# Reciprocal row sums of an attention kernel: by TensorE transposition, or over DRAM

## The chip, the cores and the metric

The kernel runs on one core of a Trainium2 chip. The metric is the device time of one execution in microseconds. The kernel before takes 977.03 us, the median of 3 runs (976.8 to 977.04).

## The reference

Causal attention with a forget gate over 4 batches, 8 heads, 576 positions and 64 channels a head, and behind it a dense mixture of 4 experts over the 2304 tokens. All is in float32.

```python
scores = scale * np.matmul(q, k.transpose(0, 1, 3, 2))
cum = np.cumsum(np.log(np.clip(f, 0.0001, 1.0)), axis=-1)
scores = np.where(causal, -1e9, scores + cum[:, :, :, None] - cum[:, :, None, :])
attn = np.exp(scores - np.max(scores, axis=-1, keepdims=True))
attn = attn / (np.sum(attn, axis=-1, keepdims=True) + 1e-09)
x = np.matmul(attn, v)                    # then heads side by side: (2304, 512)
p = domain_probs / (domain_probs.sum(-1, keepdims=True) + 1e-09)
for e in range(4):
    out += p[:, e:e + 1] * (np.maximum(x @ w1[e], 0.0) @ w2[e])
```

## The kernel before

**Tiling.** Float32 products are made of three products of parts: every operand is split into a rounded part (float32r, "hi") and its remainder ("lo"). ScalarE makes the rounded part, VectorE or GpSimd the remainder. The attention works on jobs: a job is a batch, a pair of heads and a half of the positions (half 0: the first 256 queries, in two tiles of 128; half 1: the other 320, in three tiles of 128 that begin at 256, 384 and 448, so the last two overlap by 64). There are 32 jobs, in the order of `JOBS` (line 35): batches 0 to 3 of half 0, then batches 0 to 3 of half 1, each with 4 pairs (`pr` 0 to 3). The first 4 jobs (class `First`, line 587) run in a start-up phase whose order is written out by hand (`startup`, line 1064). The other 28 are worked on while the experts' layers already run on the chunks of 256 tokens that are ready.

**Order of the work.** Each job has two heads, and the list `heads` (line 664) runs through all of them. `head_steps(n)` (line 667) lists the steps of stage n: preparation and loads for heads to come, the scores of head n tile by tile (`qk_tile`: TensorE scores, VectorE mask and row minimum of the negated scores, ScalarE exponential with the row sums), between them the transposition of the probabilities of head n-1 (`tr`: TensorE, then ScalarE's rounded copy `tr_hi` and VectorE's remainder `tr_lo`), then the product with the values (`av`). Each step has a cost, and `pace` (line 1052) deals the steps out between the quarters of the experts' steps (`Step.l1`, `Step.l2`) by these costs. Tile's scheduler then orders each engine's instructions; in the start-up phase it keeps the written order.

**The row sums.** When a pair's second head has its exponentials, `recip` (line 420) adds 1e-9 to the row sums and takes the reciprocals on VectorE; GpSimd widens them so that each stands 64 times in a row (`rb`, line 427). At the end of the next stage `fin` (line 549) calls `spread` (line 432): TensorE transposes each tile of `rb` into a PSUM tile from the pool `ps_a`, so that the reciprocal of a query stands in a column over the 64 partitions of each head. `fin` multiplies the pair's result `xs` by it (line 556, or line 579 straight into the chunk's tile `xf`), and for the chunks in `DIRECT` splits it into `xh` and `xl` (lines 562, 565). `First` uses the same `recip` and `spread` through `spread_out` (line 636), which copies the PSUM tile to SBUF.

**Places and buffers.** `place` (line 38) says which columns of a job go to which chunk of 256 tokens. `ps_a` has four slots of one bank; the scores `s`, transposed probabilities `t`, products `o` and spread sums `b` share it. All transfers of the kernel before are issued by SyncE. Lines met below: 377 scores, 391 row minimum, 406 exponential, 422 and 425 sums and reciprocals, 427 widening, 437 spreading, 465 transposition of probabilities, 475 and 482 its two copies, 515 product with the values, 595 and 608 scores and transposition of `First`, 764 and 794 the experts' two layers, 731 and 736 the split of weights, 816 the sum over experts, 914, 934 and 992 the last phase, in which 4 chunks together go through layers with seven products in place of eight (`Big`).

## Time and profile before

| what | value |
|---|---|
| median of the runs | 977.03 us |
| the profiled execution | 976.83 us |
| its span | 975.0 us |
| TensorE clock granted | 0.999 |
| TensorE busy | 963.2 us (99%) |
| VectorE busy | 657.3 us (67%) |
| ScalarE busy | 472.0 us (48%) |
| GpSimd busy | 413.0 us (42%) |
| transfers' share of 16 DMA engines | 26.8% |

The span goes from the first to the last profiled instruction; the execution's time has 1.8 us more around it. In the rows, PE is TensorE's matmuls, PEld its loads of weights into the array, DVE is VectorE, ACT ScalarE, POOL GpSimd and SP SyncE; SPq is SyncE's sequencer, which issues transfers. Records of matmuls overlap: a record's length is not the time that the next one waits. The attention's jobs after the first four take from about 27 to 560 us, the experts' sweeps go on to about 605 us, and then the last phase begins.

### The profile page before, as it was taken

Reading aid. Unit: us, or ns where it says so; the run is one execution under the profiler, and the core shown is the slowest. Engines: PE = TensorE matmul, PEld = TensorE weight load, DVE = VectorE, ACT = ScalarE, POOL = GpSimd, SP = SyncE. Lnnn points to the kernel's source line nnn. Section 1 sums busy time; section 2 is a strip of 40 time slices with the busy share of each in tenths; the row PEclk is TensorE's granted clock in tenths of the full one; section 3 lists DMA queues with packets and bytes.
Section 4 is the critical chain, followed back from the end, with each engine's and each line's share of the span. In section 5 each row is a group of like instructions: output and inputs, shape, how many; then the busy total and the mean of one; then the engine's idle time right before and its main releaser. Section 6 shows DMA issues by size and latency. Waiting matters only on the chain.

```text
span 975.0 us, 15448 instructions
## 1 busy us (share of the span) xinstructions
PE 963.2 (99%) x5690; PEld 848.1 (87%) x5690; DVE 657.3 (67%) x1349; ACT 472.0 (48%) x979; POOL 413.0 (42%) x459
## 2 busy tenths in 40 slices
PE   8999999999999999999999999999999999999998
PEld 6898999899999999999899999988788888888886
DVE  6876565777867878877777563247866666566665
ACT  7776665566556656666556353234333232323220
POOL 4987763502303202204104083477654444555410
PEclk9999999999999999999999999999999999999999
DMA  7665331332412212313412022322211112111002
GB/s 258 255 207 163 118 106 49 103 109 69 137 52 90 102 54 84 120 52 96 150 57 66 23 66 83 113 86 66 87 44 44 44 43 69 62 44 44 23 0 87
DMA packets 29819, 85.87 MB, mean 88 GB/s; under 512 B 3160, under 2 KB 5264, under 8 KB 29744
## 3 DMA queue, kind: packets, MB, share of 16 engines
q1 hardware_dynamic: 29744, 84.89, 26.8%
q8 instruction: 45, 0.74, 0.3%
q14 instruction: 30, 0.25, 0.1%
HBM read 80.00 MB, written 4.87 MB: 87 GB/s over the span
## 4 chain that ended last, share of the span: by engine, by line
PE 87%; POOL 4%; DVE 3%; issue 2%; DMA 2%; ACT 1%; POOLq 0%; ACTq 0%; DVEq 0%
PE l L764 21%; PE l L794 20%; PE y L992 17%; PE m L934 13%; PE s L377 5%; PE t L465 5%; PE o L515 5%; POOL bwl L914 2%; DMA wr<-in_w 1%; POOL wt L891 1%; PE b L437 1%; POOL wl L736 1%; DVE kl L333 1%; DVE hi L339 0%; ACT wh L731 0%
## 5 line engine op out<-in xcount | busy, mean ns | idle before, releaser
L736 POOL TENSOR_TENSOR wl<-wr,wh 128x512 fp32r<-128x512 f32 x114 | 150.3, 1344 | 76.6 <-ACT wh L731 63.0
L764 PE MATMUL l<-xl,wh 128*128 128x256 f32 x640 | 182.0, 285 | 0.3 <-DVE xl L658 0.3
L764 PE MATMUL l<-xh,wh 128*128 128x256 f32 x640 | 181.2, 284 | 0.2 <-ACT xh L657 0.2
L764 PE MATMUL l<-xh,wl 128*128 128x256 f32 x640 | 181.3, 284 | 0.0
L816 DVE SCALAR_TENSOR_TENSOR acc<-y,prob,acc 128x512 f32<-128x512 f32 x120 | 88.3, 746 | 68.5 <-PE y L992 68.5
L406 ACT ACTIVATE p<-p,nm 128x576 f32<-128x576 f32 (+2 forms) x160 | 96.0, 600 | 64.8 <-DVE nm L391 64.3
L794 PE MATMUL l<-wh,gh 128*128 128x512 f32 x320 | 127.2, 398 | 0.0
L794 PE MATMUL l<-wl,gh 128*128 128x512 f32 x320 | 127.1, 397 | 0.0
L794 PE MATMUL l<-wh,gl 128*128 128x512 f32 x320 | 126.0, 396 | 0.0
L764 PEld LDWEIGHTS l<-xh,wh 128*128 128x128 f32 x640 | 120.5, 188 | 3.2 <-ACT xh L657 0.4
L764 PEld LDWEIGHTS l<-xl,wh 128*128 128x128 f32 x640 | 120.6, 188 | 3.0 <-DVE xl L658 0.5
L764 PEld LDWEIGHTS l<-xh,wl 128*128 128x128 f32 x640 | 120.5, 188 | 0.5
L325 POOL CAST q<-raw 64x320 fp32r<-64x320 f32 (+1 forms) x56 | 26.9, 480 | 210.3 <-PE s L377 181.9
L914 POOL TENSOR_TENSOR bwl<-wr,bwh 128x256 fp32r<-128x256 f32 (+1 forms) x80 | 78.5, 1009 | 80.5 <-ACT bwh L911 80.5
L391 DVE CUSTOM_DVE_ANT_0 p<-s,mask 128x288 f32<-128x288 f32 (+2 forms) x160 | 75.6, 477 | 43.3 <-PE s L377 39.7
L992 PE MATMUL y<-bwh,hh 128*128 128x512 f32 x256 | 101.1, 395 | 0.8 <-DVE acc L816 0.8
L992 PE MATMUL y<-bwl,hh 128*128 128x512 f32 x256 | 101.1, 395 | 0.0
L992 PE MATMUL y<-bwh,hl 128*128 128x512 f32 x256 | 100.4, 395 | 0.0
L776 DVE SCALAR_TENSOR_TENSOR gl<-l,gh 128x512 fp32r<-128x512 f32 x80 | 54.9, 686 | 54.6 <-ACT gh L775 54.4
L482 DVE TENSOR_TENSOR ptl<-t,pth 128x320 fp32r<-128x320 f32 (+2 forms) x120 | 65.3, 553 | 37.0 <-ACT pth L475 36.6
L934 PE MATMUL m<-rl,bwh 128*128 128x512 f32 x224 | 87.5, 390 | 0.0
L934 PE MATMUL m<-rh,bwh 128*128 128x512 f32 x224 | 87.3, 390 | 0.0
(117 smaller groups left out, 2077.5 us busy)
## 6 DMA issues: line engine op xcount, KB each, us to landing
wr<-in_w SPq DMA_DIRECT2D x96, 512.0 KB
raw<-in_qk SPq DMA_DIRECT2D x16, 896.0 KB
raw<-in_qk SPq DMA_DIRECT2D x12, 512.0 KB
vr<-in_v SPq DMA_DIRECT2D x16, 320.0 KB
out<-acc SPq DMA_DIRECT2D x16, 256.0 KB
vr<-in_v SPq DMA_DIRECT2D x8, 128.0 KB
first<-in_qk SPq DMA_DIRECT2D x3, 256.0 KB
first<-in_v SPq DMA_DIRECT2D x4, 128.0 KB
```

The lines of the kernel that those rows point to most:

```text
L377: nc.tensor.matmul(out=ps[:, at : at + z - a], lhsT=lhsT, rhs=rhs, start=(m == 0), stop=(m == 1),)
L391: nc.vector.tensor_tensor_reduce(out=pt[:, a:z], in0=ps, in1=mask[:, m0 + a : m0 + z], scale=-0.125, scalar=BIG if n == 0 else nm[:, col : ...
L406: return nc.scalar.activation(out=pt[:, :w_], in_=pt[:, :w_], func=AF.Exp, scale=-1.0, bias=self.nmax[hh][:, c : c + 1], accum_out=self.ss ...
L482: nc.vector.tensor_tensor(out=lo[:, a0 + first : a0 + at - first], in0=ps[:, 2 * first : at], in1=hi[:, a0 + first : a0 + at - first].bitc ...
L736: eng.tensor_tensor(out=wl[n][:, a:z], in0=wraw[n][:, a:z], in1=wh[n][:, a:z].bitcast(F32), op=ALU.subtract)
L764: nc.tensor.matmul(out=self.l1p[:, fi, :], lhsT=lhsT, rhs=rhs[:, k, :], start=(k == 0 and m == 0), stop=(k == 3 and m == 2),)
L776: nc.vector.scalar_tensor_tensor(out=self.gl, in0=self.l1p, scalar=0.0, in1=self.gh.bitcast(F32), op0=ALU.max, op1=ALU.subtract,)
L794: nc.tensor.matmul(out=l2[tt], lhsT=lhsT, rhs=rhs, start=(self.ps == 0 and fi == 0 and m == 0), stop=(self.ps == 1 and fi == 1 and m == 2),)
L816: nc.vector.scalar_tensor_tensor(out=acc[c][:, tt, :], in0=ps, scalar=sc, in1=acc[c][:, tt, :], op0=ALU.mult, op1=ALU.add,)
L914: nc.gpsimd.tensor_tensor(out=lo[:, a:z], in0=x[:, a:z], in1=hi[:, a:z].bitcast(F32), op=ALU.subtract)
L934: nc.tensor.matmul(out=ps, lhsT=lhsT[:, o], rhs=rhs[:, k, :], start=(k == 0 and i == 0), stop=(k == 1 and i == 2),)
L992: nc.tensor.matmul(out=ps, lhsT=lhsT, rhs=rhs, start=(fi == 0 and m == 0), stop=(fi == 1 and m == 2),)
```

## The change

For a pair that is not the last of its group (`pr < NPR - 1`) and that belongs to neither batch 0 nor batch 1 of half 0 (`b + 4 * half > 1`), the flag `far_sums` is set. For such a pair, `recip` ends in `send` in place of `widen`: VectorE writes the reciprocals into a 128x32 tile, turns that in blocks of 32x32, and ScalarE's queue issues a transfer of it to DRAM. After the last block of transposed probabilities of the second head, `fetch` issues on ScalarE's queue a transfer from DRAM that gives every row to the 64 partitions of its head, into an SBUF tile. `fin` comes in the stage after (`head_steps`, behind the first transposition block and the first tile of scores), and multiplies by that tile. The other pairs keep GpSimd's widening and TensorE's transposition; their spread tile now has the third tile of half 1 at columns 256 to 383, so a product that runs over column 256 is made in two instructions (`scale`). `First.spread_out` calls `spread` twice. The words that came with the change speak of 20 of 28 later pairs.

```diff
--- before.py
+++ after.py
@@ -104,6 +104,7 @@
     prob = const.tile([128, NT // 128, E], F32, name="prob")
     psum_ = const.tile([128, NT // 128, 1], F32, name="psum_")
     warm = const.tile([B * H, 1], F32, name="warm")
+    rs32 = [const.tile([128, 32], F32, name=f"rs32_{n}") for n in range(2)]
     ncd = dr_p.tile([B * H, 2, S], F32, tag="ncd", name="ncd", bufs=1)
 
     scr = acc_p.tile([128, 1024], F32, tag="acc", name="scr")
@@ -166,6 +167,8 @@
             channel_multiplier=1,
         )
         make_identity(nc, ident)
+        for t in rs32:
+            nc.gpsimd.memset(t, 1.0)
         for i in jobs[1:NPR]:
             nc.gpsimd.memset(i.kq[64:65, :, :CH], 8.0)
         for t in q2:
@@ -261,6 +264,7 @@
             self.qo, self.ko = (0, CH) if half == 0 else (self.wk, 0)
             self.njt = 2 if half == 0 else 5
             self.nm = f"{b}_{pr}_{half}"
+            self.far_sums = pr < NPR - 1 and b + 4 * half > 1
             self.hi, self.kl, self.p, self.nmax = {}, {}, {}, {}
             self.sp, self.last, self.pt, self.tp, self.op = {}, {}, {}, {}, {}
 
@@ -354,7 +358,6 @@
             if hh == 0:
                 n = len(self.its)
                 self.ssum = st_p.tile([128, 2, n], F32, tag="ssum", name=f"ss{self.nm}")
-                self.rs = st_p.tile([128, 2, n], F32, tag="rs", name=f"rs{self.nm}")
 
         def qk_pe(self, hh, its):
 
@@ -422,22 +425,52 @@
             nc.vector.tensor_scalar(
                 out=self.ssum, in0=self.ssum, scalar1=1e-9, scalar2=None, op0=ALU.add
             )
-            nc.vector.reciprocal(out=self.rs, in_=self.ssum)
+            if self.far_sums:
+                self.send()
+            else:
+                self.widen()
+
+        def widen(self):
+            n = len(self.its)
+            rs = st_p.tile([128, 2, n], F32, tag="rs", name=f"rs{self.nm}", bufs=2)
+            nc.vector.reciprocal(out=rs, in_=self.ssum)
             self.rb = x_p.tile([128, 3, 2, D], F32, tag="r", name=f"rb{self.nm}")
             nc.gpsimd.tensor_copy(
                 out=self.rb[:, :n],
-                in_=self.rs.rearrange("p h i -> p i h").unsqueeze(3).to_broadcast([128, n, 2, D]),
+                in_=rs.rearrange("p h i -> p i h").unsqueeze(3).to_broadcast([128, n, 2, D]),
             )
 
         def spread(self):
 
             ps = ps_a.tile([128, 512], F32, tag="a", name=f"b{self.nm}")
             for t in self.its:
-                i, o = t - self.its[0], TOK0[t] - self.q0
+                i = t - self.its[0]
                 nc.tensor.transpose(
-                    ps[:, o : o + 128], self.rb[:, i].rearrange("p h d -> p (h d)"), ident
+                    ps[:, 128 * i : 128 * i + 128], self.rb[:, i].rearrange("p h d -> p (h d)"), ident
                 )
             self.r = ps
+
+        def send(self):
+            n, x = len(self.its), rs32[self.pr % 2]
+            nc.vector.reciprocal(
+                out=x[:, : 2 * n].rearrange("p (h i) -> p h i", h=2), in_=self.ssum
+            )
+            rt = st_p.tile([128, 32], F32, tag="rt", name=f"rt{self.nm}", bufs=2)
+            nc.vector.transpose(out=rt, in_=x)
+            self.rd = dr_p.tile([32, 4, 32], F32, tag="rd", name=f"rd{self.nm}")
+            nc.scalar.dma_start(out=self.rd.rearrange("c b r -> b c r"), in_=rt)
+
+        def fetch(self):
+            n = len(self.its)
+            self.r = x_p.tile([128, 384], F32, tag="r", name=f"r{self.nm}")
+            with tc.issue_after(self.tail.ins):
+                nc.scalar.dma_start(
+                    out=self.r[:, : 128 * n],
+                    in_=self.rd[: 2 * n]
+                    .rearrange("(h i) b r -> h (i b r)", h=2)
+                    .unsqueeze(1)
+                    .to_broadcast([2, 64, 128 * n]),
+                )
 
         def blocks(self):
 
@@ -472,7 +505,7 @@
 
         def tr_hi(self, hh, gi):
             ps, a0, first, at = self.tp[hh, gi]
-            nc.scalar.activation(
+            self.tail = nc.scalar.activation(
                 out=self.pt[hh][0][:, a0 : a0 + at - first], in_=ps[:, first:at], func=AF.Copy
             )
 
@@ -498,6 +531,8 @@
             self.tr_pe(hh, gi)
             self.tr_hi(hh, gi)
             self.tr_lo(hh, gi)
+            if hh == 1 and gi == len(self.blocks()) - 1 and self.far_sums:
+                self.fetch()
 
         def av_pe(self, hh):
             w_ = self.wq
@@ -551,11 +586,10 @@
             pieces = place(self.b, self.half)
             k = self.pr
             direct = any(p[1] in DIRECT for p in pieces)
-            self.spread()
+            if not self.far_sums:
+                self.spread()
             if direct:
-                nc.vector.tensor_tensor(
-                    out=self.xs[:, :w_], in0=self.xs[:, :w_], in1=self.r[:, :w_], op=ALU.mult
-                )
+                self.scale(self.xs, 0, w_)
             for d, c, o, n in pieces:
                 if c in DIRECT:
                     th, tl = x_tiles(c)
@@ -576,12 +610,17 @@
                             out=xf[c][:, k, o : o + n], in_=self.xs[:, d : d + n]
                         )
                     else:
-                        nc.vector.tensor_tensor(
-                            out=xf[c][:, k, o : o + n],
-                            in0=self.xs[:, d : d + n],
-                            in1=self.r[:, d : d + n],
-                            op=ALU.mult,
-                        )
+                        self.scale(xf[c][:, k, o : o + n], d, n)
+
+        def scale(self, out, d, n):
+            for a, z, o in ((d, min(d + n, 256), 0), (max(d, 256), d + n, 64)):
+                if a < z:
+                    nc.vector.tensor_tensor(
+                        out=out[:, a - d : z - d],
+                        in0=self.xs[:, a:z],
+                        in1=self.r[:, a + o : z + o],
+                        op=ALU.mult,
+                    )
 
 
     class First(Job):
@@ -634,6 +673,7 @@
                 )
 
         def spread_out(self):
+            self.spread()
             self.spread()
             self.rc = x_p.tile([128, 320], F32, tag="tmp", name=f"rc{self.nm}")
             nc.scalar.activation(out=self.rc[:, :CH], in_=self.r[:, :CH], func=AF.Copy)
@@ -691,13 +731,15 @@
             for gi in range(len(j.blocks())):
                 ts.append((500, lambda j=j, hh=hh, gi=gi: j.tr(hh, gi)))
             us.append((200 + 400 * j.half, lambda j=j, hh=hh: j.av(hh)))
-            if hh == 1:
+            if hh == 1 and not j.far_sums:
                 us.append((0, j.fin))
         if n + 1 < len(heads):
             j, hh = heads[n + 1]
             us.append((0, lambda j=j, hh=hh: j.begin(hh)))
         for k in range(max(len(qs), len(ts))):
             st += ts[k : k + 1] + qs[k : k + 1]
+            if k == 0 and n > FIRST + 1 and heads[n - 2][1] and heads[n - 2][0].far_sums:
+                st.append((0, heads[n - 2][0].fin))
         return st + us
```

## Rows read from the trace of the kernel before

**Rows 1.** The page, busy time by engine: us (share of the span) xinstructions.
```profile
PE 963.2 (99%) x5690; PEld 848.1 (87%) x5690; DVE 657.3 (67%) x1349; ACT 472.0 (48%) x979; POOL 413.0 (42%) x459
```

**Rows 2.** Busy time by stretch: stretch, its us, PE, PEld, DVE, ACT, POOL, PEclk, DMA, GB/s.
```profile
98.00:210.00 112.00, 111.29 (x773) 102.97 (x772) 71.67 (x186) 69.13 (x167) 58.63 (x72) 1.00 0.33 100
210.00:560.00 350.00, 349.52 (x2396) 324.07 (x2395) 262.81 (x635) 207.24 (x432) 75.59 (x90) 1.00 0.25 82
```

**Rows 3.** The chain that ended last, 596 to 760 us: start us, us, what.
```profile
603.97 2.08 PE l L794 x9
...
606.08 1.07 ACT wh L731
...
626.47 3.36 DMA wr<-in_w
```

**Rows 4.** Groups by form: busy us, mean ns of one, idle us before.
```profile
L437 PE MATMUL b<-ident,rb 128*128 128x128 f32 x80 | 15.2, 286 | 1.1 <-POOL rb L427 1.1
...
L425 DVE RECIPROCAL rs<-ss 128x6 f32<-128x6 f32 x16 | 3.0, 185 | 0.8
```

**Rows 5.** Timeline of PE, a block of three: start us, us, engine, line, operation.
```profile
248.46 0.55 PE L437 MATMUL b<-ident,rb 128*128 128x128 f32 x3
248.77 0.36 PE L764 MATMUL l<-xh,wl 128*128 128x256 f32 x1
248.97 0.28 PE L764 MATMUL l<-xh,wh 128*128 128x256 f32 x1
...
249.43 0.28 PE L764 MATMUL l<-xh,wl 128*128 128x256 f32 x1
249.55 0.28 PE L764 MATMUL l<-xh,wh 128*128 128x256 f32 x1
```

**Rows 6.** Timeline of PE, a block of two.
```profile
119.34 0.38 PE L437 MATMUL b<-ident,rb 128*128 128x128 f32 x2
119.55 0.38 PE L465 MATMUL t<-ident,p 128*128 128x128 f32 x2
```

**Rows 7.** Timeline of all engines in the start-up phase.
```profile
16.01 0.82 PE L595 MATMUL s<-first 65*128 65x128 f32 x4
...
17.20 0.42 DVE L391 CUSTOM_DVE_ANT_0 p<-s,mask 128x256 f32<-128x256 f32 x1
...
24.02 0.44 PE L437 MATMUL b<-ident,rb 128*128 128x128 f32 x2 [1.05 <-POOL rb L427]
```

**Rows 8.** Timeline of SP, 200 to 330 us: one issue of each kind.
```profile
202.28 0.25 SPq L295 DMA_DIRECT2D kl<-ncd  x1
...
215.91 0.55 SPq L276 DMA_DIRECT2D raw<-in_qk  x1
...
250.64 0.34 SPq L714 DMA_DIRECT2D wr<-in_w  x1
```

**Rows 9.** Timeline of SP at the start: the decay rows to DRAM and back.
```profile
14.55 0.31 SPq L200 DMA_DIRECT2D ncd<-scr  x1
...
20.17 0.53 SPq L295 DMA_DIRECT2D kl<-ncd  x2
```

**Rows 10.** The page, DMA queue: packets, MB, share of 16 engines' span.
```profile
q1 hardware_dynamic: 29744, 84.89, 26.8%
```

**Rows 11.** Timeline of all engines around one pair's sums, half 1, batch 0.
```profile
216.00 0.19 DVE L425 RECIPROCAL rs<-ss 128x6 f32<-128x6 f32 x1
...
217.06 0.62 ACT L406 ACTIVATE p<-p,nm 128x384 f32<-128x384 f32 x1 [1.13 <-DVE nm L391]
...
221.07 0.44 ACT L475 ACTIVATE pth<-t 128x320 fp32r<-128x320 f32 x1 [1.80 <-PE t L465]
...
227.69 0.55 DVE L391 CUSTOM_DVE_ANT_0 p<-s,mask 128x384 f32<-128x384 f32 x1
```

## Prediction

> **What bounds the kernel now.** I read the engines' shares first. TensorE is busy for 99% of the span; no other engine passes 67% [rows 1]. A busy TensorE need not be a bound one, so the next view is the table by stretches. The pairs that the change touches are worked on from about 98 to 560 us. There TensorE misses 0.71 us of 112 and 0.48 us of 350, at a granted clock of 1.00, which is the level of 2.4 GHz [rows 2]. VectorE is busy 64 and 75% of these two stretches, ScalarE 62 and 59%. So in this stage an end comes earlier only by taking work off TensorE, and at most 1.2 us is to be had by taking its waits away. Then I asked whether a gain made there lasts to the end. The chain of waits goes from the stage's last TensorE work at 603.97 into ScalarE's split of a weight at 606.08 [rows 3], and then through GpSimd and weight transfers (626.47): what follows starts when TensorE lets go of a buffer, so it moves forward with TensorE.
>
> **The change, part by part.** By its condition (not a chunk's last pair, and neither batch 0 nor batch 1 of the first half) the far way is taken by 6 groups of pairs times 3, which is 18 pairs and not 20: 6 of the first half with two transpositions each, 12 of the second with three, 48 transpositions in all. The other 10 later pairs and the 4 first ones keep theirs.
>
> *Taken from TensorE.* The record of such a transposition lasts 286 ns [rows 4], but records overlap, so the price is read from starts. In a block of three the first starts at 248.46 and the next matmul at 248.77, 0.31 us later; that matmul then takes 0.20 us to its successor, where the same kind further on takes 0.12 [rows 5]. So a block of three costs 0.31 + 0.08 = 0.39 us. A block of two, with another transposition behind it, costs 119.55 - 119.34 = 0.21 us [rows 6]. Sum: 12 x 0.39 + 6 x 0.21 = 4.7 + 1.3 = 6.0 us, all on the engine that sets the end. The Trainium skill ("TensorE: Matmul & The Clock Gate", Part 4) gives about 275 ns for one 128x128 transposition in a kernel's context; the record agrees and the starts do not, for three start within 0.31 us. By that figure the 48 would be 13.2 us and the time 965; the sum goes by the starts.
>
> *Added at the start.* The four first pairs now transpose twice: 8 more transpositions, and four more PSUM tiles out of the four slots that scores, transposed probabilities and spread sums share. The last of the four blocks starts at 24.02 after TensorE waited 1.05 us for the widened sums from GpSimd, and its 0.2 us lies on the path; the earlier three come out of that wait. If the slots go round in order, a fifth tile in the ring makes the scores that start at 16.01 wait for the slot of the scores before them, which VectorE reads until 17.20 + 0.42 = 17.62 [rows 7]: 1.6 us later. What hides it is again the 1.05 us before the last block, since GpSimd's queue decides when that one starts. Bounds: 0.2 us (all hidden but the last block) to 2.0 us (1.6 beside 0.4). I take 0.4, nearer the lower end, because that wait of 1.05 us is on GpSimd's queue, and its work there doesn't read these scores.
>
> *Moved to ScalarE's queue.* Each far pair issues a store of its 32 columns and a load that copies each row to 64 partitions: 36 issues. The trace has none on ScalarE; on SyncE one takes 0.25 us (the decay rows, 2 partitions), 0.34 us (a weight, 128 partitions) or 0.55 us (raw queries and keys, 128 partitions in two pieces) [rows 8]. So 36 x 0.25 to 0.55, or 9 to 20 us, of ScalarE's time over 460 us. It idles about 40% there, so this is hidden unless it stands in front of something that TensorE needs at once. Behind the store stand the next exponentials; ScalarE already waits 1.13 us at 217.06 for VectorE [rows 11]. Behind the load stand the next gate and exponentials.
>
> *VectorE.* One more instruction a pair, the turning of a 128x32 tile: nearest is the reciprocal of 128x6 at 0.19 us [rows 4]. A second-half product over column 256 is now cut in two, one more short instruction for 16 pairs, priced alike: 34 x 0.19 = 6.5 us, which VectorE's idle quarter covers; but the turning stands between the sums and the next row minimum (216.00, then the exponential at 217.06 [rows 11]), the chain that ends in TensorE's next transpositions. GpSimd loses 18 copies and gains two small fills: nothing on the path.
>
> *What ScalarE and VectorE cost TensorE.* Bounds: nothing (the 1.13 us of ScalarE's waiting in the pair of rows 11 takes the issue in) to the full chain, 0.2 us of turning plus 0.34 us of issue (the weight's, the middle one of rows 8, since store and load have 128 partitions in one piece) for every pair, 18 x 0.54 = 9.7 us. The order of all queues is made anew around the changed instructions and TensorE has other matmuls to put between, as it now does with almost no wait [rows 2], so I take 0.08 us a pair, 1.4 us.
>
> *The product a head later.* It waits for the store, then the load. The nearest row for such a round trip is the decay rows' way over DRAM at the start: store issued at 14.55, its reader not before 20.17, 5.6 us, while transfers were at their densest [rows 9]. The store is issued near 216.2, the load behind the last copy of the next head's transposed probabilities, near 221.5, and the product stands after the first tile of the head after that, near 228.2 [rows 11]. That leaves 6.7 us for the load. No SyncE issue is moved; SyncE's queue is passed by nothing. A chunk's last pair still closes at its old place, so no chunk is ready later.
>
> *Sum.* The profiled execution has a span of 975.0 and 976.83 us in all, 0.2 under the median of 977.03. 976.83 - 6.0 + 0.4 + 1.4 = 972.6; against the median 972.8.
>
> **The rivals.**
>
> *A. ScalarE late, slower.* Place: the store's issue and VectorE's turning between a pair's sums and the next exponentials. Price: the full 0.54 us a pair reaches TensorE: 976.83 - 6.0 + 0.4 + 9.7 = 980.9. It decides from the point where a pair loses more than it gains, 5.6 / 18 = 0.31 us. For it: TensorE issues in order and already runs without a gap, so nothing absorbs a late operand but the order itself. Against it: the 1.13 us of ScalarE waiting right there. Chance 0.15.
>
> *B. The load is late.* Mean packet: 26.8% of 16 x 975 us over 29744 packets is 0.14 us for 2.85 KB [rows 10]. 128 rows over 16 engines are 8 packets, 1.1 us; over two engines 64, 9.0 us. The two-engine end would land the load at 221.5 + 0.3 + 9.0 = 230.8, 2.6 us after VectorE reaches the product; VectorE idles 25% of a head's 11 us, 2.7 us, so most of that is absorbed; a quarter of it, 0.65 us for 12 pairs, adds 7.8 to the 972.6: 980.4. For the two engines speaks the Trainium skill ("DMA: Bandwidth & Descriptors", Rules for kernel authors): an outermost dimension of fewer than 16 confines a transfer to that many engines, and the load's source begins with the 2 heads; no run here shows it for this load. Against the delay: 1.5 KB rows are half the mean packet, so 64 of them take nearer 4.5 us and land before 228. Chance 0.10.
>
> *C. No gain.* The stage ends earlier but the GpSimd and transfer chain from 606 us on [rows 3] holds the old pace: 976.8. Against it, that chain starts from TensorE. Chance 0.10.
>
> *D. More gain.* 18 PSUM tiles fewer in the ring, and the 1.2 us of waits in the stage go too, with no loss on ScalarE: 976.83 - 6.0 + 0.2 - 1.2 = 969.8. Chance 0.13.
>
> *E. The records are the price:* 48 x 286 ns [rows 4] = 13.7 us off TensorE, 964.9 with the rest as forecast. Against it stand the starts of rows 5. Chance 0.02.
>
> *F. Not what it says:* the far pairs are 18, and were they 20, two more blocks of three would add 0.8 us of gain; inside the forecast.
>
> **How the numbers follow.** Forecast 972.8 with 0.50; its own range, with the start at 0.2 to 2.0 and lateness at 0 to 4 us, is 971.0 to 977. A change of 0.2%, 1.95 us, is about what a measurement can tell from none, so faster means under 975.1 and slower over 979.0. Faster: 0.46 of the forecast's 0.50, D and E: 0.61. Within: C's 0.10, 0.04 of the forecast and 0.04 of A's and B's milder shapes: 0.18. Slower: the rest of A and B: 0.21. For 8 in 10 the range goes from D's 969.8 up through the forecast and C to the milder half of A and B, to 980.0.
>
> **What would show each step.** Right: TensorE's record has 40 transpositions of sums (80 now, less 48, plus 8), about 5 us less matmul work between 98 and 560, and its idle there stays under 3 us; 36 transfers on ScalarE's queue at 0.25 to 0.55 us; the load lands within 6 us; the first weight product starts within 0.5 us of its old time. Wrong by A: TensorE idles for several us between 98 and 560 with ScalarE's exponentials or copies named as releasers. Wrong by B: VectorE waits for the load before the product. Wrong by the start: the first layer's matmuls begin over 1 us later. Wrong by C: the attention stage ends 5 us earlier and the end doesn't.

## The result, and the profile after

The changed kernel takes 986.99 us, the median of 4 runs (985.83 to 993.06), against 977.02 before: a ratio of 1.0115 (95% interval 1.008 to 1.0151). It is slower by 10 us, where 972.8 was forecast and the range ended at 980.0. The profiled execution is the longest of these runs (993.06 us, span 991.3), so its rows show where the time goes, and the sizes below come from the ratios.

The page's first part and its row for ScalarE's queue of transfers, to be read beside [rows 1] and [rows 10]:

```profile
PE 971.1 (98%) x5650; PEld 854.1 (86%) x5650; DVE 667.7 (67%) x1383; ACT 470.0 (47%) x979; POOL 405.5 (41%) x443
...
q10 hardware_dynamic: 4716, 3.44, 1.1%
```

TensorE has 40 matmuls fewer (48 transpositions removed, 8 added) and yet is busy 8 us longer. Not all of the 8 us is the change's: in this execution the granted clock was 0.50 in two stretches of 6.8 us, from about 9.5 and from about 135.8 us on, and work at half the clock makes up to 6.8 us of it (an estimate from these two lengths). VectorE has the 34 instructions more that were counted. The queue's 4716 packets are 18 pairs by 262: 128 rows stored, 128 loaded, and 6 that end a transfer, one for each engine that took part. By their records those are four engines for the store and two for the load.

Busy time by stretch, the columns of [rows 2]:

```profile
98.00:210.00 112.00, 105.56 (x708) 97.17 (x708) 77.60 (x206) 71.20 (x178) 59.12 (x69) 0.97 0.33 106
210.00:560.00 350.00, 345.69 (x2333) 319.14 (x2333) 261.60 (x643) 201.68 (x420) 68.44 (x75) 1.00 0.27 91
```

TensorE idles 6.44 and 4.31 us of these stretches, together 10.75, where it idled 1.19 before. It also does less in the same time: 708 matmuls for 773, and 2333 for 2396, though only 12 and 36 were removed from these stages. The groups of the removed and the new work answer to [rows 4]:

```profile
L448 PE MATMUL b<-ident,rb 128*128 128x128 f32 x40 | 7.1, 279 | 0.4 <-POOL rb L438 0.4
...
L459 DVE STREAM_TRANSPOSE rt<-rs 128x32 f32<-128x32 f32 x18 | 3.7, 203 | 0.2
```

So the transpositions did go, 80 to 40. What TensorE and the engines before it waited for, 98 to 605 us (total us, times, longest):

```profile
DVE xf L618 <- DMA r<-rd: 8.0, 5, 2.3
...
PE t L498 <- ACT p L409: 5.8, 5, 2.4
...
ACT p L409 <- DMA rd<-rt: 3.4, 1, 3.4
...
PE s L380 <- DVE xs L572: 2.5, 2, 2.3
ACT gh L817 <- DMA rd<-rt: 2.1, 1, 2.1
...
DVE xs L618 <- DMA r<-rd: 1.6, 2, 0.8
```

The road over DRAM is the way of the sums into DRAM and back, and both halves of it are in the list: `rd<-rt` is the store, `r<-rd` the load. For each, an engine stands that TensorE needs. (The 2.5 us for `xs` L572 are not the road's; the last section comes to them.) Timeline of one store and load of half 0 (ACTq is ScalarE's sequencer):

```profile
114.26 0.56 ACTq L461 DMA_DIRECT2D rd<-rt  x1
...
118.58 0.53 ACTq L467 DMA_DIRECT2D r<-rd  x1
...
119.16 0.40 ACT L409 ACTIVATE p<-p,nm 128x128 f32<-128x128 f32 x1 [3.39 <-DMA rd<-rt]
...
119.71 0.33 PE L498 MATMUL t<-ident,p 128*128 128x128 f32 x1 [1.92 <-ACT p L409]
```

The load may only go out when the store has landed, 4 us after its issue. ScalarE takes its queue in order: it stands 3.39 us, the exponential behind the load is late, and TensorE stands 1.92 us for it. One pair on, the same thing has another name in the list: the exponential at 135.47 waits 3.43 us, put down to a transfer of queries and keys, but the load ahead of it on ScalarE's queue goes out at 134.88, 0.4 us after the last packet of its store. And one of half 1:

```profile
354.98 0.54 ACTq L467 DMA_DIRECT2D r<-rd  x1
...
361.29 0.49 DVE L618 TENSOR_TENSOR xf<-xs,r 128x192 f32<-128x192 f32 x2 [1.74 <-DMA r<-rd]
```

VectorE gets to the product before the load has landed and stands; row minima wait behind it.

The start, beside [rows 7]. The first 27 us by the columns of [rows 2], before and below it after:

```profile
0.00:27.00 27.00, 22.51 (x118) 17.33 (x118) 17.99 (x62) 19.20 (x57) 14.41 (x28) 1.00 0.82 267
```

```profile
0.00:27.00 27.00, 24.02 (x112) 19.57 (x113) 15.82 (x58) 17.85 (x53) 12.21 (x27) 0.87 0.79 250
```

The first spreading and the first weight product before, and the same after with the last two spreadings:

```profile
15.80 0.38 PE L437 MATMUL b<-ident,rb 128*128 128x128 f32 x2
...
24.87 0.36 PE L764 MATMUL l<-xh,wh 128*128 128x256 f32 x1
```

```profile
17.99 0.60 PE L448 MATMUL b<-ident,rb 128*128 128x128 f32 x4
...
25.17 0.60 PE L448 MATMUL b<-ident,rb 128*128 128x128 f32 x4
26.19 0.66 PE L448 MATMUL b<-ident,rb 128*128 128x128 f32 x4 [0.41 <-POOL rb L438]
...
27.25 0.36 PE L806 MATMUL l<-xh,wh 128*128 128x256 f32 x1
```

The first weight product begins at 27.25, 2.4 us later than before. But TensorE comes to its first spreading 2.2 us late (17.99 for 15.80), when nothing has been doubled yet. The granted clock is 0.87 in the mean of these 27 us, where it was 1.00: this is the stretch at 0.50 from about 9.5 us on. So most of the 2.4 us is this execution's clock. A run shown below, with one spreading and the same 0.87 (load and product held), begins its first weight product at 26.75.

### The profile page after: what moved, and what is told of

It is laid out like the page before. It is cut to its first block, busy times and chain, and to the rows that moved or that the text cites. A ratio compares the mean times of both kernels' runs of the same rounds, so it can differ in the third digit from the quotient of the medians.

```text
span 991.3 us, 15453 instructions
## 1 busy us (share of the span) xinstructions
PE 971.1 (98%) x5650; PEld 854.1 (86%) x5650; DVE 667.7 (67%) x1383; ACT 470.0 (47%) x979; POOL 405.5 (41%) x443
## 3 DMA queue, kind: packets, MB, share of 16 engines
q10 hardware_dynamic: 4716, 3.44, 1.1%
## 4 chain that ended last, share of the span: by engine, by line
PE 81%; DVE 5%; DMA 4%; POOL 3%; issue 3%; ACT 2%; ACTq 0%; POOLq 0%; DVEq 0%
PE l L806 19%; PE l L836 19%; PE y L1034 16%; PE m L976 12%; PE s L380 5%; PE t L498 5%; PE o L550 4%; POOL bwl L956 2%; DMA rd<-rt 1%; DMA wr<-in_w 1%; POOL wt L933 1%; DMA r<-rd 1%; DVE rl L920 1%; PE s L634 1%; DVE v L316 1%
## 5 line engine op out<-in xcount | busy, mean ns | idle before, releaser
L976 PE MATMUL m<-rh,bwl 128*128 128x512 f32 x224 | 86.5, 390 | 0.0
```

What stands on the lines that cost most here:

```text
L976: nc.tensor.matmul(out=ps, lhsT=lhsT[:, o], rhs=rhs[:, k, :], start=(k == 0 and i == 0), stop=(k == 1 and i == 2),)
```

## The experiments

Three theories to begin with: **W**, engines stand for the store and the load; **V**, VectorE's new work or the new order of the queues; **S**, the start. Each ratio is against the kernel before on the same chip, with its 95% interval.

**The road and the start, each alone.**

```diff
# no road: store and load out
-            nc.scalar.dma_start(out=self.rd.rearrange("c b r -> b c r"), in_=rt)
...
+            self.r = r_one
# one spread, in the changed kernel
             self.spread()
-            self.spread()
# two spreads, in the kernel before
             self.spread()
+            self.spread()
```

> Left out: the store to DRAM and the load back; the 18 far pairs are multiplied by a constant tile of ones in place of their reciprocals. VectorE's turning, the product a head later, the cut products and the doubled spreading at the start all stay. Theory W (the road over DRAM: ScalarE stands before the load until the store has landed, VectorE stands before the product until the load has landed, TensorE runs dry behind them): 972 to 976 us, TensorE's idle time between 98 and 560 us back from 10.8 to under 3 us. Rival V (VectorE's added instructions and the order made anew are what costs): 983 us or more. Rival S (the doubled spreading at the start): 983 us or more.

Measured: 980.18 us, 1.0024 (1.0013 to 1.0035). The road is some 9 us of the 11, and TensorE's idle time from 98 to 560 us falls to 1.77 us, as W said. V and S alone, at 983 or more, are out. But W's 972 to 976 us are missed: with 48 transpositions fewer and no transfer at all the kernel is still not faster. (The tile of ones lies ahead of other tiles and moves them further; what that does comes below.)

> The changed kernel with one spreading per first pair, as before. W: the first weight product comes back from 27.2 to about 25 us and the time falls by 1 to 4 us, to 983 to 986. Rival S (the doubled spreading delays the start, lets the clock fall and shifts all that follows): 977 us or less. V: 984 to 987.

Measured: 987.58 us, 1.0096 (1.0071 to 1.0121). The first weight product is back at 24.94, but the time is not: W's 983 to 986 are missed as well as S's 977. S is not the cause.

> The kernel before with nothing changed but the doubled spreading of the first four pairs. W and V: 977.5 to 980 us, the first weight product 0.5 to 2.5 us later than at 24.87. S: 984 us or more.

Measured: 979.67 us, 1.0015 (0.9988 to 1.0043). By this run alone the start's doubling is worth -1 to 4 us, too wide to use: one of its ten runs took 990.40 us at a granted clock of 0.931, and the four fastest, 977.01 to 977.47, lie 0.3 to 0.8 us above the fastest of the kernel before (976.70). The first weight product begins at 26.92, but here too TensorE is late ahead of all spreading: eight score matmuls from 9.11 on take 2.90 us, where before they took 1.55. Whether the doubling makes such a slow beginning likelier is not shown.

**The product later, a first attempt.**

```diff
# load a head later, product a further head later
-            if hh == 1 and gi == len(self.blocks()) - 1 and self.far_sums:
-                self.fetch()
+            k = jobs.index(self) - 1
+            if hh == 0 and gi == len(self.blocks()) - 1 and jobs[k].far_sums:
+                jobs[k].tail = self.tail
+                jobs[k].fetch()
...
-                st.append((0, heads[n - 2][0].fin))
+                st.append((0, heads[n - 3][0].fin))
```

> The changed kernel with the load issued one head later (behind the next pair's first head's last copy) and the product one head later again, so that the store has landed long before ScalarE reaches the load, and the load before VectorE reaches the product. All instructions are the same ones. W: 972 to 977 us, no wait of ScalarE over 1 us before a load, TensorE's idle time between 98 and 560 us under 4 us. V and S: 983 us or more.

Measured: 1005.0 us, 1.0277 (1.0246 to 1.0308). The trace of this run says why. First its waits on the load's tile, then one load and the product behind it:

```profile
  DMA r<-rd: 56.8, 17
```

```profile
225.77 0.54 ACTq L467 DMA_DIRECT2D r<-rd  x1
...
231.65 0.56 DVE L620 TENSOR_TENSOR xs<-xs,r 128x256 f32<-128x256 f32 x2 [3.42 <-DMA r<-rd]
```

The product stands right behind the load in 17 of 18 pairs, 56.8 us of standing against 9.6 in the changed kernel. The place of `fin` in the code doesn't fix its place on VectorE's queue: the queues are ordered anew by a scheduler, and it put the product there. (That it expects the load to land sooner than it does would explain the place, but no run shows it.) W's 972 to 977 could not be tried in this way. As a dose this run is useful: 47 us more of VectorE's standing made the time 18 us longer.

**The place in SBUF.** The run without the road left some 5 us unexplained, with weight products starting a little further apart (281 ns for 280) also after the attention had ended. The tiles that the change adds move the tiles behind them by 448 bytes a partition.

```diff
# shift: kernel before, one unused tile
+    pad = const.tile([128, 112], F32, name="pad")
...
# placed: changed kernel, new tiles behind all others
+    sm_p = AT("sm", 1)
+    rs32 = [sm_p.tile([128, 32], F32, name=f"rs32_{n}") for n in range(2)]
```

> The kernel before with one tile more that nothing uses, 448 bytes a partition among the constants, so that every tile behind it on that side of SBUF lies where the changed kernel has it; no instruction of the loop is changed (one more GpSimd fill at the start). Theory P (place): the runs so far left about 5 us unexplained in the run without the road, whose weight products start a little further apart than before (median of one 281 ns against 280, of a score 307 against 296, of an output product 397 against 395), also where nothing else differs, after the attention has ended; the tiles that the change adds have moved TensorE's operands. Then 979.5 to 982. Theory N (no effect of place; the order of the work, or VectorE's additions, slow the products): 976.8 to 977.6.

Measured: 982.56 us, 1.0058 (1.0042 to 1.0074). P holds, by 5.7 us; the profiled executions are 3.7 us apart (spans of 978.7 and 975.0). The page and the stretches of the shifted kernel:

```profile
PE 967.9 (99%) x5690; PEld 853.2 (87%) x5690; DVE 657.6 (67%) x1349; ACT 473.3 (48%) x979; POOL 413.5 (42%) x460
```

```profile
98.00:210.00 112.00, 111.37 (x769) 103.29 (x770) 71.60 (x186) 68.72 (x168) 59.22 (x73) 1.00 0.32 99
210.00:560.00 350.00, 349.58 (x2382) 324.09 (x2380) 262.63 (x632) 208.02 (x431) 75.52 (x89) 1.00 0.25 82
```

The same 5690 matmuls take 967.9 us for 963.2, and TensorE idles no more than in [rows 2] (1.05 us for 1.19): no wait has changed, only the matmuls' pace. By groups, 3.9 of the 4.7 us are in the products of the experts' first layer (548.4 us for 544.5). The scores' longer median, which the expectation named, was not a sign of it: the shifted kernel's groups of scores last what they did before.

> The changed kernel with its new tiles in a pool of their own behind all others, so that every other tile lies where the kernel before has it; nothing else is changed. P: 2 to 5 us less than the changed kernel, 982 to 985. N: 986 to 988, as the changed kernel. W (the road's waits) says nothing on it by itself, the road is untouched.

Measured: 983.98 us, 1.0065 (1.0052 to 1.0078): 3.0 us less than the changed kernel by the medians, 4.9 by the ratios (into which the run of 993.06 goes). P again.

> Store and load left out (the far pairs are multiplied by ones), tiles placed as in the kernel before, single spreading at the start: what is left of the change is 48 transpositions fewer on TensorE, the VectorE transpositions and the product a head later. P: the removal then pays what its starts cost, 48 by 0.11 = 5.3 us: 971.5 to 973.5. N: still no gain, 977 to 979 (the run without the road had 980.2, the doubled spreading cost up to 2.5).

Measured: 975.43 us, 0.9976 (0.9968 to 0.9985). The removal pays 2.3 us, between P and N; in the profiled execution 3.2 (span 971.8 against 975.0). It is faster than the kernel before, but leaves the row sums out. It also settles V: VectorE's new instructions and an order made anew are all in it, and no time is lost. Against the placed kernel with the road and one spreading (1.0058, below) the whole road costs 8.2 us. The page's first part, the stretches, and VectorE's groups:

```profile
PE 959.4 (99%) x5642; PEld 843.0 (87%) x5642; DVE 668.1 (69%) x1383; ACT 472.1 (49%) x979; POOL 405.8 (42%) x444
```

```profile
98.00:210.00 112.00, 111.68 (x775) 103.15 (x774) 82.56 (x213) 73.07 (x180) 58.18 (x67) 1.00 0.34 108
210.00:560.00 350.00, 349.43 (x2376) 322.89 (x2375) 265.79 (x647) 207.07 (x426) 71.38 (x78) 1.00 0.24 79
```

```profile
L609 DVE TENSOR_TENSOR xs<-xs,r_one 128x256 f32<-128x256 f32 x9 | 5.9, 661 | 0.0
...
L609 DVE TENSOR_TENSOR xs<-xs,b 128x256 f32<-128x256 f32 x7 | 2.9, 419 | 0.2
```

TensorE's matmuls take 3.8 us less in sum (959.4 for 963.2), and it idles 0.89 us from 98 to 560. The same product lasts 661 ns in the mean with its factor in SBUF and 419 with it in PSUM; five of the nine in SBUF take 411 to 421 ns too, so it is the others that are long, up to 1514.

> The whole road kept, tiles placed as before, single spreading; the load is issued a head later, when the store has landed (12 us after its issue in the run that did this alone, where ScalarE did not stand), and the product stands at the end of the head after that, some 10 us behind the load instead of right behind it. W with P: neither engine waits for a transfer any more, 972 to 975. W with N: 977 to 980. If the longer life of the unscaled product's tile holds something up: over 985, and the waits name the tile.

Measured: 1007.6 us, 1.0306 (1.0288 to 1.0324). The product was again moved up behind the load, and VectorE stood 60.8 us in 17 pairs. Neither theory was tried by it.

**The product held.** A dependence on a VectorE instruction of a later head (`j.lo`, the last remainder of the transposed probabilities) now fixes the place.

```diff
+                    with tc.issue_after(self.then.ins) if self.far_sums else ExitStack():
                         nc.vector.tensor_tensor(
...
+                us.append((0, lambda i=i, j=j: i.end(j.lo)))
```

> Tiles placed as before, single spreading, store and load where the change has them; the product is queued on VectorE behind the last transposed scores of the next head, so that it comes some 5 to 10 us after the load has landed. In the two runs that meant to do this it still stood 0.5 us behind the landing in 17 of 18 pairs, because the order on an engine is made anew by the scheduler, not taken from where the code stands. Base: 975.4 (no road at all, same placing). Theory W, in two parts: W1 VectorE's stands before the load, W2 ScalarE's stands before the store has landed. If W1 is most of the road's 6 to 8 us: 976 to 978.5. If W2 is: 979.5 to 982.5, hardly less than the 984.0 of the changed kernel placed as before.

Measured: 977.73 us, 1.0002 (0.9991 to 1.0013): W1. What is left of the road's waits from 98 to 560 us:

```profile
PE t L499 <- ACT p L410: 3.7, 4, 1.9
ACT p L410 <- DMA rd<-rt: 3.4, 1, 3.4
...
ACT gh L823 <- DMA rd<-rt: 1.9, 1, 1.9
...
DVE xs L624 <- DMA r<-rd: 1.5, 2, 1.0
```

ScalarE still stands for the store about as long as in the changed kernel (3.4 and 2.1 us there), VectorE 1.5 us in place of 9.6, and the time is back at that of the kernel before.

> As the run before it in this list, and the load is issued a head later and the product held a head later too: neither engine stands. W1 or W2 alike: 975 to 977.5. Rival X (the road costs by its presence, issues on ScalarE and transfers beside SyncE's, not by stands): 980 or more, though the waits on the transfers are gone.

Measured: 976.6 us, 0.9994 (0.9982 to 1.0005). No engine stands for the load, and ScalarE once for a store:

```profile
ACT gh L825 <- DMA rd<-rt: 1.1, 1, 1.1
```

This is the best version with the whole road; by the interval it can't be told from the kernel before. Six of its 12 runs (975.51 to 976.24) lie under the lowest of the 25 of the kernel before (976.70), so a small gain is possible and not shown.

```diff
# load by SyncE, product held
-            with tc.issue_after(self.tail.ins):
-                nc.scalar.dma_start(
+            with ExitStack():
+                nc.sync.dma_start(
```

> Product held as in the first of this list, the load issued by SyncE instead of ScalarE, so that ScalarE no longer stands for the store; SyncE's transfers of weights and inputs queue behind the load. W2: 975 to 977.5. If SyncE's own transfers become late instead: 980 or more, with waits on in_w or in_qk.

Measured: 979.85 us, 1.0026 (1.001 to 1.0042). This is just under the second reading's 980, and its sign is there: weight transfers of SyncE's became late, for which ScalarE stands 6.9 us (0.8 with the load on ScalarE's own queue). Waits of this run, 98 to 560 us:

```profile
ACT wh L779 <- DMA wr<-in_w: 6.9, 2, 4.4
...
PE o L551 <- ACT pth L509: 3.3, 1, 3.3
```

```diff
# wide load: one transfer per head
-                    out=self.r[:, : 128 * n],
+                for h in range(2):
...
+                        out=self.r[64 * h : 64 * h + 64, : 128 * n],
```

> The changed kernel placed as before, double spreading, with the load as two transfers of 64 partitions each, one per head, so that its rows spread over all DMA engines; one issue more on ScalarE per pair (18 by 0.54 us). It has 984.0 to beat. If the two-engine load is what VectorE stands for (rival B of the prediction): the load lands in 2 to 3 us, 979 to 982. If the issue on ScalarE and the store decide: 984 to 986.

Measured: 982.94 us, 1.0052 (1.0038 to 1.0067), between the two readings. By the packets' records the load lands 2.2 to 2.6 us after its second issue in 13 of 18 pairs, and VectorE never stands for it, and yet only 1.3 us came back of W1's 5.

**The square.** Placed as before, in all four corners: spreading double or single, product held or not.

> The changed kernel placed as before, with the single spreading at the start; product where the scheduler puts it, right behind the load. Placed with the double spreading it took 984.0, with the product held and the single one 977.7: 6.3 us for two edits. If the held product is the larger share (VectorE's stand, W1): 981.5 to 984. If the start is: 978 to 980.

Measured: 984.25 us, 1.0058 (1.0044 to 1.0073).

> The other corner of the same square: product held, double spreading, placed as before. W1: 978 to 980.5, the start's doubling being worth 0 to 2.5. If the start is the larger share: 981.5 to 984.

Measured: 979.51 us, 1.0012 (1.0 to 1.0025). Holding the product gives 5.2 us with the double spreading (1.0065 to 1.0012) and 5.5 with the single one (1.0058 to 1.0002). The doubling costs 0.7 and 1.0 us, neither clear of the intervals. Stretches of the placed kernel, and below them of the same one with the product held:

```profile
98.00:210.00 112.00, 108.39 (x742) 99.92 (x741) 80.54 (x214) 73.94 (x184) 58.90 (x69) 0.98 0.37 114
210.00:560.00 350.00, 346.54 (x2349) 320.26 (x2348) 261.46 (x643) 201.62 (x420) 69.12 (x76) 1.00 0.27 88
```

```profile
98.00:210.00 112.00, 108.74 (x741) 99.91 (x741) 83.64 (x214) 73.08 (x182) 58.38 (x69) 0.98 0.35 111
210.00:560.00 350.00, 349.16 (x2370) 322.29 (x2369) 262.06 (x644) 205.08 (x423) 68.23 (x76) 1.00 0.27 90
```

The gain is in the second halves: TensorE's idle time there falls from 3.46 to 0.84 us, with 21 matmuls more done.

> Product held, single spreading, and the load as two transfers of 64 partitions. The held product left VectorE 1.5 us of standing before two loads, the wide load none: if these stands are the last of the road's cost, 975.5 to 977; if the second issue on ScalarE (18 by 0.54 us) costs what the stands did, 977.5 to 979.

Measured: 981.75 us, 1.0034 (1.0021 to 1.0047), slower than both readings and 3.1 us slower than with the product held alone. So the wide load costs something of its own, which fits that it gave back so little alone. It differs by the second issue on ScalarE (18 by 0.54 us) and by rows spread over all the engines; which of the two costs was not tried. So the wide load alone doesn't settle W1; that rests on the four corners.

**Is there a version under both?** The road for the second halves alone, then with the load held too, then with the product on GpSimd.

```diff
-            self.far_sums = pr < NPR - 1 and b + 4 * half > 1
+            self.far_sums = pr < NPR - 1 and half == 1
...
# product on GpSimd
-                        nc.vector.tensor_tensor(
+                        (nc.gpsimd if self.far_sums else nc.vector).tensor_tensor(
```

> Product held, single spreading, placed as before, and the road for the 12 far pairs of the second halves alone; the 6 of the first halves keep their transpositions, 12 more on TensorE (12 by 0.11 = 1.3 us). Between 98 and 210 us, where the first halves are, the run with the held product had 108.4 us of TensorE's work in 112 us against 111.3 before: 2.9 us of idle time there, next to none between 210 and 560. If the road pays where heads are long and costs where they are short: 977.7 + 1.3 - 2.9 gives 974.5 to 977, under both kernels. If the idle time of that stage has other causes: 977.5 to 979.

Measured: 981.49 us, 1.0032 (1.0015 to 1.005), slower than both readings.

> The road for the 12 pairs of the second halves alone, with the load and the product both held a head later; tiles placed as before, single spreading. The run with the road for the second halves and only the product held missed its 974.5 to 977: ScalarE stood 7.0 us for two stores there (4.5 at the longest), TensorE 2.2 us for the exponentials behind one of them, and its granted clock was 0.51 just after. If those stands (W2) were the miss: no wait on the store or the load is left, TensorE is idle under 1.5 us from 98 to 560, and 36 transpositions fewer at 0.11 us give 973 to 975, under both kernels. If the 12 pairs cost something else: 976.5 to 979.

Measured: 979.69 us, 1.0025 (1.0009 to 1.0042), again slower than both readings; its 12 runs lie between 976.27 and 983.71 at granted clocks of 1.000 to 0.991. No wait for the store or the load is left in its trace. TensorE still idles 4.01 us from 98 to 560; its one long wait, for a row minimum, comes first here, and below it what VectorE and GpSimd do ahead of it:

```profile
PE s L381 <- DVE nm L395: 3.3, 2, 2.9
```

```profile
528.91 5.13 POOL L786 TENSOR_TENSOR wl<-wr,wh 128x512 fp32r<-128x512 f32 x4 [5.53 <-ACT wh L781]
...
530.25 3.87 DVE L626 TENSOR_TENSOR xf<-xs,r 128x64 f32<-128x64 f32 x3
```

Three products, usually 0.2 to 0.4 us each, last 3.87 us and end when GpSimd's run does. Sorting all these products by whether GpSimd works beside them: those that read the sums from PSUM always keep their usual length; those that read both operands from SBUF keep it while GpSimd rests, and are longer beside it, by 1.9 us in sum in the changed kernel and by 7.8 in the run with load and product held (up to 2.9 us for one product).

> Road for all 18 far pairs, load a head later, tiles placed as before, single spreading; the far pairs' products move from VectorE to GpSimd. In the traces so far the product of two SBUF operands takes its usual 0.2 to 0.4 us on VectorE while GpSimd rests and up to 2.9 us while GpSimd works (12 of 39 products ran beside it in the run with both held, 7.9 us over their usual length; none of the products that read PSUM was stretched, in any run). Theory G (that stretch is what is left of the road's cost at 976.6): with the product on GpSimd's own queue no product is stretched and VectorE never stands for a load, 973.5 to 975.5, under both kernels. Rival: GpSimd, standing for the load and slower at the product, makes weight parts or the next heads' queries late: 977.5 or more, with waits on GpSimd's lines.

Measured: 987.97 us, 1.0092 (1.0077 to 1.0108): the rival. GpSimd stands for the loads; the dependence on a VectorE instruction, which is in this edit too, did not keep its products behind them. For the largest group:

```profile
L626 POOL TENSOR_TENSOR xs<-xs,r 128x256 f32<-128x256 f32 x9 | 6.6, 736 | 57.6 <-DMA r<-rd 54.6 <-DMA vr<-in_v 3.0
```

So no version with the road is shown to beat the kernel before, and the stretch is seen but its share of the time is not isolated.

## Why the prediction was wrong

Against the kernel before, the 10 to 11 us divide like this by the ratios, each difference uncertain by 1 to 2 us or more: removal of the transpositions with all that goes with the product -2.3; the road's presence, with the product and the load held, +1.8 (0.9976 to 0.9994); the load's early issue, +0.8 (inside the intervals); the product's place, with VectorE's stands for the load, +5.2 to 5.5; the doubled start, +0.7 to 1.0; the place of the tiles, +3.0 to 5.7.

*Taken from TensorE.* The count was right (18 pairs, 48 transpositions, 40 left). The price of 6.0 us was read from starts, and only 2.3 came back (1.5 to 3.1 by the interval), 3.2 in the profiled execution. So this term was about twice too large. Why stays open: without the road TensorE doesn't stand for operands (0.89 us idle from 98 to 560), and its matmuls' sum fell by 3.8 us, 0.08 us for each of the 48, where the starts gave 0.13.

*Moved to ScalarE's queue.* The issues take 0.54 us, in the bounds. But "hidden unless it stands in front of something that TensorE needs at once" priced the issue and not the wait before it: the load may not go out before the store has landed, and that was 1.6 us only in a few pairs and 2.3 to 6.3 in most, by the packets' records. The text named what is queued behind the store and the load, but set no wait there. What the stands cost by themselves is small, 0.8 us and inside the intervals, if one goes by the load issued a head later.

*The product a head later.* This is the step that failed most. "the product stands after the first tile of the head after that, near 228.2 ... That leaves 6.7 us for the load" took one pair's distance for that of all 18. VectorE comes to the product 3.7 to 12 us after the load's issue; 6.7 is near the middle of the 18, but in 7 pairs the load came later than VectorE, which stood 9.6 us. With the product held behind a later instruction 5.2 to 5.5 us came back. And "64 of them take nearer 4.5 us and land before 228" was too short: by the packets' records the loads of half 1 land 5.3 to 8.5 us after their issue. For the two engines the rule of the Trainium skill ("DMA: Bandwidth & Descriptors", Rules for kernel authors) that rival B cited holds: two packets end each load.

*What ScalarE and VectorE cost TensorE.* 1.4 us was taken from bounds of 0 and 9.7; measured, with the stands, 7 to 8.2. The lower part was chosen because the order left almost no wait before. That was no reason: the order was made for operands that were there.

*Added at the start.* 0.4 us from bounds of 0.2 to 2.0; measured 0.7 to 1.0, inside the bounds and within the noise. The 2.4 us of the profiled execution are mostly its clock: TensorE was 2.2 us late ahead of the first spreading. The prediction's sign for this step, a first weight product over 1 us late, would have misled here.

*VectorE.* "0.19 us" for the turning was right (203 ns). That the product changes from a PSUM operand to two SBUF operands was not seen at all.

*Not in the sum.* The place of the tiles, 3 to 6 us of a miss of 14, has no step in the prediction.

*Rivals.* B came true in its mechanism: VectorE stands for the load, priced at 7.8 us and measured at 5.2 to 5.5. A's sign is in the trace, 5.8 us of TensorE for exponentials, but ScalarE is late for the store's landing and not by the issue's length, and the share that is its own is 0.8 to 2.6 us (early issue and presence of the road) where A said 9.7. The two were held apart, at 980.9 and 980.4 with chances of 0.15 and 0.10, as if one excluded the other.

## What to carry to other kernels

A transfer that waits for another on a compute engine's queue is a wait of that engine: price the standing, not the issue, and look at the queue's real order, since a scheduler may put the reader right behind its load. One pair's distances are not those of all pairs. Before a time is laid to an edit, give the edit's new tiles a place where they move nothing, or shift the old kernel alike: here up to half of the loss came from 448 bytes. A price read from starts is not yet what comes back: 6.0 us were priced here and 2.3 to 3.2 measured, and the cause is open. And before a late start is laid to an edit, look at the granted clock ahead of it.

## What the runs showed of the hardware

**Place in SBUF.** Moving the weights', chunks' and other tiles by 448 bytes, with every instruction of the loop the same, made TensorE's matmuls 0.5% longer in sum (967.9 us for 963.2) and the kernel 0.58% slower (0.42 to 0.74). Most of it is in the experts' first layer; which operand's place matters was not tried.

**VectorE beside GpSimd.** A VectorE product of two SBUF operands was stretched from 0.2 us to as much as 2.9 while GpSimd worked (load and product held), one with a PSUM operand never. The Trainium skill ("SBUF — State Buffer", Who interferes with whom) says that a VectorE instruction with two SBUF inputs contends with a GpSimd instruction that reads SBUF, because its second input comes through the shared read interface. The traces agree: in the lines above three products last 3.87 us beside GpSimd's 5.13 us of weight remainders. The prediction should have used it.

**The granted clock after a stand.** In the profiled execution TensorE stood 2.41 us before 136.12, for the exponential that was behind the load. Stretches before and after, with the granted clock in the third column from the end:

```profile
129.00:135.80 6.80, 4.71 (x33) 4.06 (x32) 2.90 (x9) 1.70 (x5) 0.87 (x2) 1.00 0.54 183
135.80:142.60 6.80, 6.48 (x26) 6.00 (x27) 5.18 (x15) 4.57 (x14) 3.42 (x6) 0.50 0.12 37
```

For 6.8 us, from about 0.4 us before the end of the stand on, the clock was 0.50, which is the level of 1.2 GHz; in these stages the kernel before has 1.00 throughout [rows 2]. Another stand of 2.31 us, which ended at 348.99, was followed by no such stretch. (It was not the road's: a VectorE remainder, L343, usually 0.49 us, took 3.11 us ahead of `xs` while GpSimd worked.) So a stand may cost more than its length: 2.41 us here and, if the fall came of it, up to half of 6.8 behind it, an estimate from the two levels. The fastest of the changed kernel's runs, 985.83 us, had a mean granted clock of 0.999, the slowest, 993.06, one of 0.993. Runs of the kernel before spread in the same way, from 976.70 us at 1.000 to 981.29 at 0.994, and a difference of 1 or 2 us between two kernels is to be read with that in mind.
